# First batch of an attention and two-layer kernel: VectorE's work in one fixed order

## The chip, the cores and the metric

The kernel runs on one core of a Trainium2 chip. The metric is the device time of one execution in microseconds (us). Before the change it is 1152.64 us, the median of three runs (1151.52 to 1152.75). One further execution was recorded by the hardware profiler; all rows below are from it.

The engines carry short names in the rows: PE is TensorE (PEld its weight loads), DVE is VectorE, ACT is ScalarE, POOL is GpSimd, SP is the engine that issues most DMAs.

## What is computed

```
q, k, v: 4 batches x 8 heads x 576 x 64;  tau = 0.02
scores = q @ k^T / 8
keep only scores >= row maximum - tau        (all others: -1e9)
attn = exp(scores - row maximum) / (row sum + 1e-9)
x = attn @ v, heads side by side:            2304 x 512
x = (silu(x @ w_gate) * (x @ w_val)) @ w_out   512 -> 1536 -> 512
out = relu(x @ w_in)^2 @ w_out2                512 -> 2048 -> 512
```

Everything is float32. Most products are made from split operands: a rounded high part and the rest, in three matmuls per product.

## The kernel before, in words

The attention is cut into 144 tiles of 128 query rows by 576 keys: 4 batches, 4 pairs of heads, 9 tiles for a pair. Tiles 0 to 35 are the first batch. In the first batch PE has nothing but the attention; from tile 36 on, the matmuls of the first layer of the batch that is done ("fill") are put between the attention's.

One tile goes through these steps, which the code names by functions:

- QK: four matmuls (eight for the fifth tile of a pair) write the scores `s` into one of two PSUM buffers.
- RED (L623, DVE): the row maximum minus tau, `thr`, read from PSUM.
- CUT (L631, ACT): writes `z` from `s` and `thr`; there is one `z` buffer.
- EXP (L639, ACT): `e = exp(z)` and its row sum. An accumulator read of the same line follows it.
- RCP (L644, DVE): the reciprocal of the sum; NORM (L649, POOL): `e` times it.
- TR (L669, PE): five 128x128 transposes of `e` into two PSUM banks, three columns in one and two in the other.
- PH (L55 in the first batch): copies them to SBUF, one bank by DVE and the other by ACT ("evacuation"). In later batches it is L689 on ACT with a subtraction L61 on DVE.
- AV (L725 in the first batch, L728 later): the product with the values, four times in nine tiles.

Beside this the first layer's weights, which arrive as 64-bit floats, are brought into split 32-bit form: 30 pieces of 128 x 256. A piece takes one step on ACT (L137), four on DVE (L139, L141, L145, L147, each reading what the one before wrote), a copy on ACT (`wa` or `wx`, L53) and a subtraction on POOL (L61). The raw data lies in three buffers, so that three pieces can be under way. A new piece's DMA is started every second tile in the first batch, and every tile later. Twenty pieces carry gate and value weights, the last ten the output weights; the fill needs 20 pieces by its fifth unit and all 30 before its first output (around tile 56).

Each pair of heads also has its q and k split: two conversions on ACT (`land`, L559 and L53), L565 on DVE, two subtractions on POOL; and chunks `xs_m` of the first layer's input are split, L53 on ACT and L61 on DVE.

What sets the order: the program's loop over tiles issues the steps in a written sequence, each through `at_`, which gives it a priority offset from a table ("early0" for the first batch). A scheduler then fixes one order for each engine at build time; on the chip every engine works its list in that order and waits at an instruction whose inputs are missing. In the loop before, the DVE steps of the weights (`loader.tick("D")`, named LD) stand at four places of an iteration, and up to four can be issued in it.

## Time and profile before

| | |
|---|---|
| median of three runs | 1152.64 us |
| the profiled execution | 1153.14 us, of which the recorded span is 1151.3 us |
| DVE busy over the span | 874.8 us (76%) |
| PE busy over the span | 1115.7 us (97%) |
| first batch (tile 0's maximum to tile 36's) | 7.24 to 102.74 us |

A busy share over the whole span mixes stages with different limits, so the views below are cut by stretches of tiles. "Busy" of an engine counts the time in which an instruction of it is recorded as running; this takes in time in which a running instruction is held up. In a timeline row the bracket at the end, where there is one, gives the idle time before the instruction and what ended it.

### The profile page before, as it was taken

The page shows a single profiled execution, that of the slowest core. Times are in us where ns is not written, and L with a number is a line of the kernel's source. Part 1 is how long each engine was busy: PE and PEld are TensorE (multiplying, and loading weights), DVE is VectorE, ACT ScalarE, POOL GpSimd, SP SyncE. Part 2 cuts the span into 40 slices and gives each one's busy share as a digit, 9 for nine tenths or more (in the row PEclk, how much of TensorE's full clock was granted, in tenths as well). Part 3 has the DMA queues.
Part 4 walks back from the last instruction along what each step waited for, and adds up shares of the span by engine and source line. Part 5 has one row for each costly group of instructions (what it writes and reads, how often), then busy time and mean ns, then how long its engine had stood idle before and what let it go on. Part 6 is the DMA issues. An engine that isn't in the chain of part 4 may idle for free.

```text
span 1151.3 us, 19654 instructions
## 1 busy us (share of the span) xinstructions
PE 1115.7 (97%) x6572; PEld 1011.6 (88%) x6572; DVE 874.8 (76%) x2143; ACT 689.2 (60%) x1626; POOL 242.8 (21%) x363
## 2 busy tenths in 40 slices
PE   7888999999999999999999999989999999999998
PEld 5766989999999999998888888889898998899997
DVE  7999997877877773889986888668648767866554
ACT  7988988988888883554443444235546555543221
POOL 5565664555455531000000000000000000000000
PEclk9999999999999999999999999989999999999999
DMA  6666433443333400332220234246364445444542
GB/s 195 193 178 166 128 99 95 100 120 95 95 95 95 105 22 1 101 93 82 83 74 1 73 131 161 91 143 244 137 210 174 174 157 177 153 155 138 187 171 80
DMA packets 55827, 143.15 MB, mean 124 GB/s; under 512 B 7600, under 2 KB 8880, under 8 KB 55728
## 3 DMA queue, kind: packets, MB, share of 16 engines
q1 hardware_dynamic: 55584, 141.92, 39.8%
q8 instruction: 52, 0.85, 0.3%
q14 instruction: 47, 0.39, 0.1%
q10 hardware_dynamic: 144, 0.00, 0.0%
HBM read 93.06 MB, written 22.28 MB: 100 GB/s over the span
## 4 chain that ended last, share of the span: by engine, by line
PE 76%; DVE 12%; ACT 5%; DMA 2%; issue 2%; POOL 0%; POOLq 0%; DVEq 0%; ACTq 0%; SPq 0%
PE mm L226 17%; PE mm L1453 17%; PE mm L1400 13%; PE mm L271 8%; PE bank L226 6%; PE bank L669 4%; PE s L613 4%; PE bank L271 4%; PE bank L728 4%; DVE st__101 L623 2%; DMA wr<-in_w_dram 1%; ACT z L631 1%; DVE pt L61 1%; ACT e L639 1%; DVE xs_m L61 1%
## 5 line engine op out<-in xcount | busy, mean ns | idle before, releaser
L669 PE MATMUL bank<-ident,e 128*128 128x128 f32 x720 | 165.4, 275 | 10.2 <-DVE x L55 3.8
L649 POOL TENSOR_SCALAR e<-e,r 128x576 f32<-128x576 f32 x144 | 113.4, 787 | 148.1 <-DVE r L644 104.6
L61 DVE TENSOR_TENSOR pt<-bank,pt 128x384 fp32r<-128x384 f32 x216 | 100.3, 486 | 51.1 <-ACT pt L689 49.9
L226 PE MATMUL mm<-xs,wa 128*128 128x512 f32 (+2 forms) x672 | 125.7, 347 | 0.5 <-ACT x L53 0.5
L226 PEld LDWEIGHTS mm<-xs,wa 128*128 128x128 f32 x672 | 109.5, 188 | 15.7 <-ACT x L53 0.7
L631 ACT ACTIVATE z<-s,thr 128x576 f32<-128x576 f32 x144 | 106.8, 742 | 26.5 <-DVE st__101 L623 18.5
L623 DVE TENSOR_SCALAR_CACHE_REDUCE st__101<-s,tau_c 128x576 bf16<-128x576 f32 x144 | 116.6, 810 | 5.2 <-PE s L613 4.2
L669 PEld LDWEIGHTS bank<-ident,e 128*128 128x128 f32 x720 | 96.4, 141 | 21.7 <-DVE x L55 5.9
L226 PE MATMUL bank<-xs_m,wa 128*128 128x288 f32 x576 | 109.7, 327 | 3.7 <-DVE xF L740 1.8
L689 ACT ACTIVATE pt<-bank 128x384 fp32r<-128x384 f32 x216 | 88.7, 436 | 21.5 <-PE bank L669 20.2
L639 ACT ACTIVATE e<-z 128x577 f32<-128x577 f32 x144 | 99.6, 692 | 1.5 <-POOL e L649 0.4
L226 PEld LDWEIGHTS bank<-xs_m,wa 128*128 128x128 f32 x576 | 89.0, 189 | 7.1 <-DVE xs_m L61 2.7
L728 PE MATMUL bank<-pt,vs 128*128 128x256 f32 (+1 forms) x480 | 92.1, 323 | 2.1 <-ACT pt L689 1.4
L613 PE MATMUL s<-kh,qs 128*128 128x288 f32 x256 | 78.1, 319 | 7.4 <-ACT nident L413 5.9
L728 PEld LDWEIGHTS bank<-pt,vs 128*128 128x128 f32 x480 | 73.9, 190 | 3.8 <-ACT pt L689 2.1
L1470 DVE TENSOR_TENSOR xF<-xF,mm 128x512 f32<-128x512 f32 x54 | 37.0, 686 | 50.9 <-PE mm L1453 50.9
L226 PE MATMUL mm<-xs,wb 128*128 128x512 f32 (+1 forms) x360 | 74.9, 368 | 0.0
L613 PE MATMUL s<-kl,qs 128*128 128x288 f32 x256 | 73.7, 301 | 0.0
L226 PEld LDWEIGHTS mm<-xs,wb 128*128 128x128 f32 x360 | 62.9, 188 | 11.3
L53 ACT ACTIVATE wb<-wf 128x256 fp32r<-128x256 f32 x82 | 34.0, 414 | 64.5 <-DVE wf L1057 38.4
L1054 ACT ACTIVATE wf<-wr 128x256 f32<-128x256 f32 x64 | 27.6, 433 | 68.6 <-DMA wr<-in_w_dram 51.0
L1453 PE MATMUL mm<-wb,wx 128*128 128x512 f32 x270 | 67.1, 389 | 0.0
(156 smaller groups left out, 2603.0 us busy)
## 6 DMA issues: line engine op xcount, KB each, us to landing
wr<-in_w_dram SPq DMA_DIRECT2D x106, 256.0 KB, 2.9
raw<-in_qkv_dram SPq DMA_DIRECT2D x15, 896.0 KB, 4.7
kh<-land SPq DMA_DIRECT2D x60, 144.0 KB, 2.6
kl<-raw SPq DMA_DIRECT2D x60, 144.0 KB, 2.8
xF<-in_w_dram SPq DMA_DIRECT2D x30, 256.0 KB, 2.9
right<-kept1T SPq DMA_DIRECT2D x8, 768.0 KB, 5.3
right<-kept0T SPq DMA_DIRECT2D x7, 768.0 KB, 5.3
right<-kept SPq DMA_DIRECT2D x6, 768.0 KB, 5.1
```

The source lines that it names most:

```text
L61: e.tensor_tensor(out, a, b, op=ALU.subtract)
L226: mm(pt[:, :n], w[:, a, col + c * P : col + (c + 1) * P], xs[:, b, c, :], start=(i == 0), stop=(i == len(TERMS) - 1),)
L271: mm(pt[:, :n], w[:, a, 2 * DM + m * P : 2 * DM + (m + 1) * P], u[:, b, :], start=(k == 0), stop=(k == last),)
L613: mm(sp[:, cols], l, r[:, cols], start=(n_ == 0), stop=(n_ == len(pairs) - 1),)
L623: red = nc.vector.tensor_scalar(st_, st[t]["s"][:, :S], scalar1=tau_c, scalar2=None, op0=ALU.subtract, op1=ALU.max, accum_out=th)
L631: nc.scalar.activation(z[:, :S], st[t]["s"][:, :S], AF.Prelu, bias=st[t]["thr"], scale=-1.0, alpha=1 / SLOPE)
L639: ex = nc.scalar.activation(e, st[t]["z"], AF.Exp, scale=-SLOPE, accum_out=sum_)
L649: nc.gpsimd.tensor_scalar(e, e, scalar1=r, scalar2=1.0, op0=ALU.mult, op1=ALU.mult)
L669: mm(dst[:, j], e[:, c0 : c0 + P], ident, is_transpose=True, start=(j == 0), stop=(j == len(cols) - 1),)
L728: mm(o[:, :n], hd["vs"][:, SLOT[k % 5], :], pt[:, k, lo : lo + n], start=(k == 0), stop=(k == 9))
L1400: mm(bank[:, :BK], w[:, a, c * P : (c + 1) * P], t[:, b, c, :], start=(n == 0 and x in ("11", "12", "S1")), stop=(n == 5), skip_group_chec ...
L1453: mm(pt, u[:, b, s * P : (s + 1) * P], w[a], start=(half == 0 and j == 0 and i == 0), stop=(half == 1 and j == 1 and i == 2),)
```

## The change

For iterations 9 to 37 of the loop over tiles, the DVE steps are chained: each of them is issued after the DVE instruction that was traced before it (`inorder`). The written sequence of such an iteration i is: reciprocal of tile i-1, maximum of tile i, evacuation of tile i-3, two weight steps. The other places of LD are left out in these iterations. Outside of them the loop is as it was; the priorities are the same.

```diff
+    order = {"after": None}
+
+    def inorder(f, *args, name=None):
+
+        if order["after"] is None:
+            at_(f, *args, name=name)
+        else:
+            with tc.issue_after(order["after"]):
+                at_(f, *args, name=name)
+        traced = nc.cur_bb.bb.instructions
+        engine = st[0]["red"].engine
+        order["after"] = next(x for x in reversed(traced) if x.engine == engine)
+
     for i in range(NTILE + lag + 1):
...
-        at_(loader.tick, "D", name="LD")
-        if i < NTILE:
-            at_(RED, i)
+        fixed = cfg["fixed"][0] <= i < cfg["fixed"][1]
+        if fixed:
+            inorder(RCP, i - 1)
+            at_(NORM, i - 1)
+            inorder(RED, i)
             at_(CUT, i)
-        if 0 <= t < NTILE:
-            at_(PH, t)
-            at_(NEG, t)
-        if i < NTILE:
+            inorder(PH, t)
             at_(EXP, i)
-        at_(loader.tick, "D", name="LD")
+            for _ in range(2):
+                inorder(loader.tick, "D", name="LD")
+        else:
...
-        if 0 <= i - 1 < NTILE:
+        if 0 <= i - 1 < NTILE and not fixed:
             at_(RCP, i - 1)
             at_(NORM, i - 1)
-        at_(loader.tick, "D", name="LD")
+        if not fixed:
+            at_(loader.tick, "D", name="LD")
...
-        at_(loader.tick, "D", name="LD")
+        if not fixed:
+            at_(loader.tick, "D", name="LD")
...
+    "fixed": (9, 38),
```

What the scheduler makes of it is shown at three places of DVE's list. In these rows `thr7` is the maximum of tile 7, `r7` the reciprocal of its sum; the copies into `x2` are evacuations; rows from `xF` to `xF` or with `wf2` at L139 to L147 are weight steps (the three raw buffers lie in `xF`).

The first place is DVE from the maximum of tile 5 on. Before:

```order
L623 TENSOR_SCALAR st__101,thr5_257<-s1_109,tau_c_60 128x576
L139 TENSOR_SCALAR xF_64<-xF_64 128x256
L141 TENSOR_SCALAR xF_64<-xF_64 128x256
L145 SCALAR_TENSOR_TENSOR xF_64<-xF_64 128x256
L644 RECIPROCAL r4_264<-sum4_237 128x1
L147 SCALAR_TENSOR_TENSOR xF_64<-xF_64 128x256
L139 TENSOR_SCALAR wf2_80<-wf2_80 128x256
L623 TENSOR_SCALAR st__101,thr6_278<-s0_108,tau_c_60 128x576
L644 RECIPROCAL r5_285<-sum5_262 128x1
L55 COPY x2_65<-bank0_84 128x3x128
```

Now:

```order
L623 TENSOR_SCALAR st__101,thr5_257<-s1_109,tau_c_60 128x576
L644 RECIPROCAL r4_264<-sum4_237 128x1
L623 TENSOR_SCALAR st__101,thr6_278<-s0_108,tau_c_60 128x576
L644 RECIPROCAL r5_285<-sum5_262 128x1
L55 COPY x2_65<-bank0_84 128x3x128
L623 TENSOR_SCALAR st__101,thr7_298<-s1_109,tau_c_60 128x576
```

The weight steps between the maxima of tiles 5 and 7 are gone; the first weight step now stands behind the maximum and the evacuation of tile 12's iteration. Up to the maximum of tile 5 the two lists are the same.

The second place is DVE in the middle of the first batch. Before, tiles 16 to 18:

```order
L623 TENSOR_SCALAR st__101,thr16_546<-s0_108,tau_c_60 128x576
L55 COPY x2_65<-bank0_84 128x2x128
L623 TENSOR_SCALAR st__101,thr17_587<-s1_109,tau_c_60 128x576
L644 RECIPROCAL r15_555<-sum15_529 128x1
L55 COPY x2_65<-bank1_85 128x3x128
L139 TENSOR_SCALAR wf2_80<-wf2_80 128x256
L61 TENSOR_TENSOR xs_m00_1277<-xF_64,xs_m00_1277 128x288
L141 TENSOR_SCALAR wf2_80<-wf2_80 128x256
L644 RECIPROCAL r16_594<-sum16_551 128x1
L145 SCALAR_TENSOR_TENSOR wf2_80<-xF_64,wf2_80 128x256
L147 SCALAR_TENSOR_TENSOR wf2_80<-xF_64,wf2_80 128x256
L139 TENSOR_SCALAR xF_64<-xF_64 128x256
```

Now, tiles 18 and 19:

```order
L644 RECIPROCAL r17_609<-sum17_593 128x1
L623 TENSOR_SCALAR st__101,thr18_612<-s0_108,tau_c_60 128x576
L55 COPY x2_65<-bank0_84 128x3x128
L139 TENSOR_SCALAR xF_64<-xF_64 128x256
L141 TENSOR_SCALAR xF_64<-xF_64 128x256
L644 RECIPROCAL r18_648<-sum18_617 128x1
L623 TENSOR_SCALAR st__101,thr19_651<-s1_109,tau_c_60 128x576
L55 COPY x2_65<-bank0_84 128x2x128
L145 SCALAR_TENSOR_TENSOR xF_64<-xF_64 128x256
L147 SCALAR_TENSOR_TENSOR xF_64<-xF_64 128x256
```

Before, two maxima stand close together and the reciprocal of the earlier tile often behind the later tile's maximum, with a run of weight steps after them. Now every maximum stands right behind the reciprocal of the tile before it, and two steps of one piece stand behind each evacuation.

The third place is DVE where the fixed iterations end. Before, from the reciprocal of tile 35:

```order
L644 RECIPROCAL r35_1153<-sum35_1124 128x1
L623 TENSOR_SCALAR st__101,thr36_1144<-s0_108,tau_c_60 128x576
L55 COPY x2_65<-bank0_84 128x3x128
L623 TENSOR_SCALAR st__101,thr37_1186<-s1_109,tau_c_60 128x576
L55 COPY x2_65<-bank1_85 128x2x128
L644 RECIPROCAL r36_1195<-sum36_1149 128x1
L139 TENSOR_SCALAR xF_64<-xF_64 128x256
L141 TENSOR_SCALAR xF_64<-xF_64 128x256
L145 SCALAR_TENSOR_TENSOR xF_64<-xF_64 128x256
```

Now, from the reciprocal of tile 36:

```order
L644 RECIPROCAL r36_1182<-sum36_1151 128x1
L623 TENSOR_SCALAR st__101,thr37_1185<-s1_109,tau_c_60 128x576
L55 COPY x2_65<-bank1_85 128x2x128
L145 SCALAR_TENSOR_TENSOR xF_64<-xF_64 128x256
L139 TENSOR_SCALAR xF_64<-xF_64 128x256
L147 SCALAR_TENSOR_TENSOR xF_64<-xF_64 128x256
L141 TENSOR_SCALAR xF_64<-xF_64 128x256
L145 SCALAR_TENSOR_TENSOR xF_64<-xF_64 128x256
L55 COPY x2_65<-bank0_84 128x3x128
L644 RECIPROCAL r37_1221<-sum37_1190 128x1
L147 SCALAR_TENSOR_TENSOR xF_64<-xF_64 128x256
L623 TENSOR_SCALAR st__101,thr38_1212<-s0_108,tau_c_60 128x576
```

Here the run of weight steps is longer than it was before. Counted over the whole list: ahead of the maximum of tile 38 there were 22, 22, 22 and 21 instructions of L139, L141, L145 and L147, and now there are 15 of each; ahead of the maximum of tile 57 there are 30 of each in both lists. From there on DVE's and PE's lists agree apart from a few neighbouring rows up to tile 60, and wholly after that.

## Rows read from the trace of the kernel before

**Rows 1.** Page, part 1: busy time, share of the span, instructions.

```profile
PE 1115.7 (97%) x6572; PEld 1011.6 (88%) x6572; DVE 874.8 (76%) x2143; ACT 689.2 (60%) x1626; POOL 242.8 (21%) x363
```

**Rows 2.** Stretches between maxima: length; busy of PE, PEld, DVE, ACT, POOL; clock, DMA.

```profile
10.26:17.01 6.75, 5.69 (x29) 5.25 (x29) 4.68 (x13) 6.25 (x15) 4.67 (x6) 1.00 0.49 180
17.01:28.39 11.38, 10.93 (x65) 8.98 (x65) 10.85 (x31) 10.71 (x28) 6.97 (x10) 1.00 0.70 162
28.39:109.55 81.16, 69.69 (x399) 55.87 (x400) 76.38 (x199) 72.68 (x180) 48.15 (x67) 1.00 0.67 185
109.55:170.64 61.09, 57.34 (x418) 54.19 (x418) 58.38 (x154) 52.92 (x133) 38.74 (x55) 1.00 0.44 115
170.64:400.00 229.36, 226.03 (x1720) 220.21 (x1719) 177.66 (x484) 198.80 (x491) 121.92 (x180) 1.00 0.41 99
```

**Rows 3.** Timeline (start, length, engine, line): the maxima of tiles 9 and 38.

```profile
28.39 0.81 DVE L623 TENSOR_SCALAR_CACHE_REDUCE st__101<-s,tau_c 128x576 bf16<-128x576 f32 x1
...
109.55 0.81 DVE L623 TENSOR_SCALAR_CACHE_REDUCE st__101<-s,tau_c 128x576 bf16<-128x576 f32 x1
```

**Rows 4.** Timeline of VectorE and ScalarE: one tile from reciprocal to reciprocal.

```profile
102.66 0.16 DVE L644 RECIPROCAL r<-sum 128x1 f32<-128x1 f32 x1
102.74 0.80 DVE L623 TENSOR_SCALAR_CACHE_REDUCE st__101<-s,tau_c 128x576 bf16<-128x576 f32 x1
...
103.46 0.55 DVE L55 COPY x<-bank 128x384 f32<-128x384 f32 x1
...
103.64 0.74 ACT L631 ACTIVATE z<-s,thr 128x576 f32<-128x576 f32 x1 [0.17 <-DVE st__101 L623]
...
104.47 0.69 ACT L639 ACTIVATE e<-z 128x577 f32<-128x577 f32 x1
...
105.28 0.16 DVE L644 RECIPROCAL r<-sum 128x1 f32<-128x1 f32 x1 [0.20 <-ACT e L639]
```

**Rows 5.** Timeline of ScalarE: two pairs of CUT and EXP.

```profile
31.12 0.74 ACT L631 ACTIVATE z<-s,thr 128x576 f32<-128x576 f32 x1
...
32.06 0.67 ACT L639 ACTIVATE e<-z 128x577 f32<-128x577 f32 x1
...
59.20 0.74 ACT L631 ACTIVATE z<-s,thr 128x576 f32<-128x576 f32 x1
59.96 0.69 ACT L639 ACTIVATE e<-z 128x577 f32<-128x577 f32 x1
```

**Rows 6.** Lines of ScalarE, 28.39 to 109.55: a pair's conversions.

```profile
L559 ACT ACTIVATE land<-raw,qscale 128x576 fp32r<-128x576 f32 x3 | 2.3, 774 | 0.0
L53 ACT ACTIVATE land<-raw 128x576 fp32r<-128x576 f32 x3 | 2.1, 688 | 0.0
```

**Rows 7.** Timeline of VectorE and GpSimd: a weight piece beside a normalization.

```profile
62.20 0.41 DVE L145 SCALAR_TENSOR_TENSOR wf<-xF,wf 128x256 int32<-128x256 int32 x1
...
78.73 0.28 DVE L139 TENSOR_SCALAR xF<-xF 128x256 f32<-128x256 f32 x1
...
78.99 0.88 POOL L649 TENSOR_SCALAR e<-e,r 128x576 f32<-128x576 f32 x1 [1.21 <-DVE r L644]
...
79.04 0.29 DVE L141 TENSOR_SCALAR xF<-xF 128x256 int32<-128x256 int32 x1
...
79.37 0.77 DVE L145 SCALAR_TENSOR_TENSOR xF<-xF 128x256 int32<-128x256 int32 x1
...
80.17 0.43 DVE L147 SCALAR_TENSOR_TENSOR xF<-xF 128x256 int32<-128x256 int32 x1
```

**Rows 8.** Stretches, VectorE's L139, L141, L145, L147 alone, in this order.

```profile
109.55:170.64 61.09, 3.16 (x8) 1.00 0.44 115
109.55:170.64 61.09, 4.18 (x8) 1.00 0.44 115
109.55:170.64 61.09, 6.21 (x9) 1.00 0.44 115
109.55:170.64 61.09, 3.88 (x9) 1.00 0.44 115
```

More of the change, by code (lines that the diff above doesn't have):

```diff
@@ L852, in attention_moe @@
             at_(loader.start, name="LS")
-        at_(loader.tick, "D", name="LD")
-        if i < NTILE:
-            at_(RED, i)
+        fixed = cfg["fixed"][0] <= i < cfg["fixed"][1]
[3 more added lines that the diff above has]
+            inorder(RED, i)
             at_(CUT, i)
-        if 0 <= t < NTILE:
-            at_(PH, t)
-            at_(NEG, t)
-        if i < NTILE:
+            inorder(PH, t)
             at_(EXP, i)
-        at_(loader.tick, "D", name="LD")
+            for _ in range(2):
+                inorder(loader.tick, "D", name="LD")
+        else:
+            at_(loader.tick, "D", name="LD")
+            if i < NTILE:
+                at_(RED, i)
+                at_(CUT, i)
+            if 0 <= t < NTILE:
+                at_(PH, t)
+                at_(NEG, t)
+            if i < NTILE:
+                at_(EXP, i)
+            at_(loader.tick, "D", name="LD")
         at_(loader.tick, "A", name="LA")
@@ L868, in attention_moe @@
                 avq.append(t)
-        if 0 <= i - 1 < NTILE:
+        if 0 <= i - 1 < NTILE and not fixed:
             at_(RCP, i - 1)
             at_(NORM, i - 1)
-        at_(loader.tick, "D", name="LD")
+        if not fixed:
+            at_(loader.tick, "D", name="LD")
         at_(mp1.flush, "A", name="FA")
@@ L894, in attention_moe @@
                 at_(next, steps, name="PS")
-        at_(loader.tick, "D", name="LD")
+        if not fixed:
+            at_(loader.tick, "D", name="LD")
     while avq or not fstate["end"]:
```

## The prediction

> **What bounds the kernel now.** I read the page's engine totals first, then the stretches between chosen maxima, and last the timeline of single tiles. The totals give PE 97% busy and DVE 76% [rows 1]. That average hides two stages. The stretches in [rows 2] are cut where the maxima (L623) of tiles 2, 5, 9, 38 and 57 start; the columns after the length are the busy times of PE, PEld, DVE, ACT and POOL. From 170.64 on PE is busy 226.03 of 229.36 us: PE sets the pace, DVE is busy 177.66. Ahead of that DVE is the fullest engine: 10.85 of 11.38 us from tile 5 to 9, 76.38 of 81.16 from tile 9 to 38, 58.38 of 61.09 from tile 38 to 57. In the last of these PE is busy 57.34, so both are near their limit there. The lists of the engines are the same again soon after tile 57, and PE then has no room to catch up. So the change is worth what it moves the start of tile 57.
>
> Why DVE is so full is seen in single rows [rows 7]. A weight step L145 took 0.41 us at 62.20, but 0.77 at 79.37: a normalization ran on POOL from 78.99 to 79.87, and the step ended 0.27 us after it. L139 and L141, which had started before it or just with it, took 0.28 and 0.29. A step that meets a POOL operation is held until that one ends.
>
> **The change, part by part.** I price three stretches.
>
> *Tiles 5 to 9.* The weight steps that stood here are gone (the first place of the lists), 3 to 4 of each line. DVE then no longer sets the pace. The nearest rows for tiles without weight steps are tiles 2 to 5: 6.75 us for three, 2.25 a tile [rows 2]. The other end is a tile that waits for the whole chain of the one before, 2.62 (next paragraph), as tile 9 does. I take the middle, 2.43: four tiles in 9.7 instead of 11.38 us, **-1.7** (bounds -2.4 and -0.9).
>
> *Tiles 9 to 38.* Two things happen here. The DVE work falls: 15 pieces instead of 18 to 19, and few of them are held, because POOL's normalization now runs under the maximum and the evacuation. The normalization that a reciprocal sets free lasts about 0.9 us [rows 7]; in that time DVE now does the maximum and the evacuation, 0.80 and 0.55 long [rows 4], and these read PSUM and are not held. The other thing is a new wait. The list now says reciprocal of tile i-1, then maximum of tile i. The reciprocal needs EXP of tile i-1, that needs its CUT, that needs its maximum. So each round is one closed ring through DVE and ACT, and a maximum can no longer be done ahead, as it was before. The ring is read from one tile [rows 4]: reciprocal 102.66, maximum 102.74, CUT 103.64, EXP 104.47, next reciprocal 105.28, which is 0.08 + 0.90 + 0.83 + 0.81 = 2.62 us. The shortest step from CUT to EXP is 0.76 (59.20 to 59.96), which would make the ring 2.55; with another ACT instruction between the two it is 0.94 (31.12 to 32.06) [rows 5].
>
> Under the ring DVE has room: from the start of a maximum to the next reciprocal there are 2.54 us, and maximum, evacuation and two steps of 0.28 + 0.29 or 0.41 + 0.43 [rows 7] need 0.80 + 0.55 + 0.84 = 2.2 at most. So the weight steps are covered by ACT's CUT and EXP, and what was DVE's bound turns into the ring's. What waits behind a late reciprocal is the next maximum, and with it CUT, EXP and the transposes of the next tile.
>
> 29 rounds at 2.62 are 76.0 us. In 11 of them ACT's new list has an instruction between CUT and EXP: 11 x (0.94 - 0.83) = 1.2. From the end of EXP (104.47 + 0.69) to the next CUT (105.28 + 0.08 + 0.90) ACT has 1.1 us a round; its evacuations and weight copies fit, the three pairs' conversions of 0.77 and 0.69 [rows 6] together with these don't. I allow 0.4 us for each of four such rounds and 0.6 for each of the three rounds in which L565 stands between the weight steps, 3.4 in all. That gives 80.6 us against 81.16 [rows 2]: **-0.6**. The ends are 29 x 2.55 = 74.0 (-7.2), and 2.80, the present pace, plus 0.15 a round for waits of PE that the ring doesn't show (+4.3).
>
> *Tiles 38 to 57.* What was left out has to be made up here: all 30 pieces are done by tile 57 in both lists, and at tile 38 there are 15 now where there were 22. That is 27 more weight steps, 6.75 pieces, on the engine that is busy 58.38 of 61.09 us. In this stretch the four lines took 3.16/8, 4.18/8, 6.21/9 and 3.88/9 us [rows 8], 2.04 us a piece. Neighbours that don't depend on one another overlap, as reciprocal and maximum do by 0.08 us [rows 4], so that a piece occupies about 1.7 (2.04 - 4 x 0.08): 6.75 x 1.7 = 11.5. DVE's idle time in the stretch is 2.7 us; I let half of it be filled: **+10.1**. Bounds: a piece of steps that are never held is 0.28 + 0.29 + 0.41 + 0.43 = 1.41 [rows 7], and with all idle time filled 9.5 - 2.7 = +6.8; at 2.04 with none of it filled +13.8. The same pieces bring their ACT copies and POOL subtractions; ACT is busy 52.92 and POOL 38.74 of the 61.09 us, so these lie beside DVE's work. The raw data's DMAs are started by SP when a buffer comes free; in the first batch that is later than before, and three pieces are still under way at any time, so I cost them at nothing. If a load were late for a step, DVE would stand behind it, some tenths of a microsecond a piece.
>
> *Sum.* -1.7 - 0.6 + 10.1 = +7.8 us on the profiled execution's 1153.14 (the span of 1151.3 and 1.8 around it), which is 1160.9. The profiled execution is 0.5 above the median of the runs, so the forecast is **1160 us**, slower by 0.7%.
>
> [...]
>
> **The rivals.**
>
> *Faster.* The relief counts and the repayment is cheap. Rounds at the shortest ring with one instruction between CUT and EXP in 11 of them, 74.0 + 1.2: -6.0. Tiles 5 to 9 at 2.25: -2.4. Added steps that stand in one run behind the same POOL operation are held once and not four times: +6.8, and a third of that, 2.3, lies in time in which DVE would be held anyway. Sum -3.9: 1148.7. For it: DVE's 76.38 us contain much time in which steps were held. Against it: the ring is a sum of dependent steps and none of them gets shorter, and DVE is 96% busy where the steps go. 13%.
>
> *No change.* Rounds at 2.62 with only the 1.2 us added (-4.0), tiles 5 to 9 at -2.4, late weights at +6.8: +0.4, 1153.0. 16%.
>
> *Much slower.* PE's list puts an AV of some 2.5 us and five transposes ahead of the scores of the tile after next. If such a product waits for an evacuation that now comes only behind the maximum, the scores come late and the ring stands still. At the upper end above, 2.95 a round, the sum is -1.7 + 4.3 + 10.1 = +12.7: 1165.3. It decides from where a round with an AV needs more than the 5.2 us of two rings. For it: PE is busy 69.69 of 81.16 us in this stretch. Against it: the scores have two buffers and may be a tile early. 13%.
>
> That the order isn't what the change says is no rival here; the lists show it.
>
> **How the numbers follow.** Forecast 58%, with a range of its own from 1155 to 1165. A difference of 0.2%, 2.3 us, is about what a measurement of this kernel can tell from none. Faster by more than that has 13%, within it 16%, slower 71% (58 and 13). The range from 1150 to 1167 leaves out most of the faster rival and the outer part of the slowest one.
>
> **What the next profile would show.** Tile 9's maximum near 26.7 instead of 28.39 [rows 3]. From there rounds of 2.6 to 2.9 us, each reciprocal ended by a wait for ACT's EXP, DVE with idle time in every round (below 80% busy) and L145 mostly at 0.41. Tile 38's maximum near 107, against 109.55 [rows 3]. From tile 38 to 57 some 71 us, DVE as full as before with 15 pieces in place of 8, and PE with new waits for DVE. Then the same pace as before. I am wrong if tile 57 comes before 168.3: because the rounds run below 2.55, which would break the ring, or because the stretch after tile 38 takes the added steps at less than 1 us a piece.

## The result and the profile after

The changed kernel takes 1167.8 us (median of 4 runs, 1166.9 to 1168.5) against 1152.1 us (1151.2 to 1152.8) on the same chip: 1.36% longer, ratio 1.0136 with a 95% interval from 1.0119 to 1.0154. That is +15.7 us where +7.8 was forecast: 0.8 us above the wider range of 1150 to 1167, and 2.8 above the forecast's own, 1155 to 1165. The profiled execution took 1166.85 us, 1165.0 of it the span. Its totals, the answer to [rows 1], hardly show where the time went:

```profile
PE 1122.8 (96%) x6572; PEld 1013.8 (87%) x6572; DVE 873.2 (75%) x2143; ACT 691.5 (59%) x1626; POOL 240.8 (21%) x363
```

The stretches do. These are cut, as in [rows 2], where the maxima of tiles 2, 5, 9, 38 and 57 start; behind the length are PE, PEld, DVE, ACT, POOL, the granted clock, the DMA share and GB/s:

```profile
10.27:17.59 7.32, 6.44 (x29) 5.93 (x29) 4.86 (x13) 6.03 (x14) 4.45 (x6) 1.00 0.44 145
17.59:27.73 10.14, 9.78 (x57) 8.07 (x58) 5.04 (x18) 9.63 (x25) 4.76 (x8) 1.00 0.61 129
27.73:114.13 86.40, 73.58 (x410) 57.76 (x409) 69.08 (x185) 71.69 (x171) 42.20 (x61) 0.98 0.55 152
114.13:185.59 71.46, 62.12 (x417) 55.81 (x417) 70.04 (x182) 58.16 (x149) 45.50 (x63) 0.98 0.46 132
185.59:415.00 229.41, 226.47 (x1726) 220.91 (x1725) 178.29 (x486) 199.42 (x492) 122.18 (x182) 1.00 0.40 99
```

Against [rows 2]: tile 5 starts 0.58 later (the two lists are the same up to there, and in the runs told below it starts anywhere from 16.7 to 18.1, so this is not put down to the change); tiles 5 to 9 take 10.14 instead of 11.38, **-1.2**; tiles 9 to 38 take 86.40 instead of 81.16, **+5.2**; tiles 38 to 57 take 71.46 instead of 61.09, **+10.4**; from there to the end it is 1.2 less. Together +13.7, the difference of the two spans. The maxima that answer to [rows 3], and that of tile 57:

```profile
27.73 0.82 DVE L623 TENSOR_SCALAR_CACHE_REDUCE st__101<-s,tau_c 128x576 bf16<-128x576 f32 x1
...
114.13 0.81 DVE L623 TENSOR_SCALAR_CACHE_REDUCE st__101<-s,tau_c 128x576 bf16<-128x576 f32 x1
...
185.59 0.81 DVE L623 TENSOR_SCALAR_CACHE_REDUCE st__101<-s,tau_c 128x576 bf16<-128x576 f32 x1
```

The ring is there, as in [rows 4]. In the timeline of tile 27 each step waits for the one before, and the round takes 2.64 us:

```profile
81.38 0.80 DVE L623 TENSOR_SCALAR_CACHE_REDUCE st__101<-s,tau_c 128x576 bf16<-128x576 f32 x1
...
82.28 0.74 ACT L631 ACTIVATE z<-s,thr 128x576 f32<-128x576 f32 x1 [0.77 <-DVE st__101 L623]
...
83.06 0.69 ACT L639 ACTIVATE e<-z 128x577 f32<-128x577 f32 x1
...
83.94 0.16 DVE L644 RECIPROCAL r<-sum 128x1 f32<-128x1 f32 x1 [0.48 <-ACT e L639]
84.02 0.80 DVE L623 TENSOR_SCALAR_CACHE_REDUCE st__101<-s,tau_c 128x576 bf16<-128x576 f32 x1
```

Eleven of the 29 rounds are like it, 2.62 to 2.66 us. The others reach 4.1, and the mean is 2.98; in the kernel before, the time from one maximum to the next ran from 1.06 to 5.91, with a mean of 2.80. I added up, over all 29 rounds, what each of the ring's four steps took beyond the forecast's 0.90, 0.83, 0.81 and 0.08:

```
us beyond 29 x 2.62 = 76.0   CUT late  to EXP  reciprocal late  next maximum   sum
forecast's allowances           1.6      1.2        1.8             -           4.6
changed kernel                  2.9      2.3        4.9            0.4         10.4
```

Two long rounds show how it comes about. In round 26 (timeline) a copy on ACT stands ahead of CUT, and itself waits for PE's transposes; another stands between CUT and EXP; the reciprocal then starts only behind one more copy of ACT, which the profile names as what it waited for:

```profile
78.66 0.38 ACT L53 ACTIVATE x<-bank 128x256 f32<-128x256 f32 x1 [0.78 <-PE bank L669]
...
78.94 0.73 ACT L631 ACTIVATE z<-s,thr 128x576 f32<-128x576 f32 x1
...
79.74 0.43 ACT L53 ACTIVATE xF<-bank 64x320 f32<-64x320 f32 x1
...
80.07 0.67 ACT L639 ACTIVATE e<-z 128x577 f32<-128x577 f32 x1
...
81.30 0.16 DVE L644 RECIPROCAL r<-sum 128x1 f32<-128x1 f32 x1 [1.35 <-ACT x L53]
```

In round 30 (VectorE's timeline) EXP had long been done, and the reciprocal stands behind three steps that were held while POOL worked without a break from 90.67 to 93.63:

```profile
90.87 0.69 DVE L139 TENSOR_SCALAR xF<-xF 128x256 f32<-128x256 f32 x1
91.48 1.43 DVE L565 SCALAR_TENSOR_TENSOR raw<-raw,qscale,land 128x576 fp32r<-128x576 f32 x1
92.83 0.95 DVE L141 TENSOR_SCALAR xF<-xF 128x256 int32<-128x256 int32 x1
93.70 0.15 DVE L644 RECIPROCAL r<-sum 128x1 f32<-128x1 f32 x1
```

L565 takes 0.82 us at 64.25, where POOL is idle (0.00 us busy from 64 to 66), and 1.43 here.

Such holds did not become few in tiles 9 to 38. The maximum and the evacuation now cover POOL's normalization, but POOL's subtraction for a weight piece (L61) follows it and meets the first weight step. L139, 0.28 us when free, took 0.63 in the mean of its 15 rows; 12 of them were over 0.5, and all 12 started after such a subtraction, or one of a pair's, had started and before it ended:

```profile
L139 DVE TENSOR_SCALAR xF<-xF 128x256 f32<-128x256 f32 x10 | 6.7, 670 | 0.0
L139 DVE TENSOR_SCALAR wf<-wf 128x256 f32<-128x256 f32 x5 | 2.7, 545 | 0.0
```

A whole piece took 1.94 us of DVE here, against 2.06 in the kernel before.

Round 37 (4.01 us) is another thing: behind it the fixed order ends, and five weight steps stand ahead of the reciprocal of tile 37 in DVE's list (the third place of the lists). It holds 1.4 of the 10.4 us, and it is 4.0 to 4.2 us long in seven of the other ten runs with a ring too.

The waits of tiles 9 to 38 (us in all, times, longest) name, among others, the ring, PE's transposes behind DVE's evacuations, and ACT's copies behind PE's transposes:

```profile
DVE r L644 <- ACT e L639: 17.1, 22, 1.9
ACT z L631 <- DVE st__101 L623: 8.4, 15, 1.1
...
PE bank L669 <- DVE x L55: 5.3, 7, 1.6
...
ACT x L53 <- PE bank L669: 1.6, 4, 0.8
```

### The profile page after: what moved, and what is told of

Read it like the earlier page. It is cut to its first block, busy times and chain, and to the rows that moved or that the text cites. A ratio compares the mean times of both kernels' runs of the same rounds, so it can differ in the third digit from the quotient of the medians.

```text
span 1165.0 us, 19639 instructions
## 1 busy us (share of the span) xinstructions
PE 1122.8 (96%) x6572; PEld 1013.8 (87%) x6572; DVE 873.2 (75%) x2143; ACT 691.5 (59%) x1626; POOL 240.8 (21%) x363
## 4 chain that ended last, share of the span: by engine, by line
PE 80%; DVE 9%; ACT 4%; DMA 4%; issue 2%; POOL 0%; SPq 0%; POOLq 0%; ACTq 0%; DVEq 0%
PE mm L226 17%; PE mm L1479 17%; PE mm L1426 13%; PE mm L271 9%; PE bank L226 6%; PE bank L669 5%; PE s L613 4%; PE bank L271 4%; PE bank L728 4%; PE bank L725 2%; DVE st__101 L623 2%; DVE pt L61 1%; ACT z L631 1%; DMA raw<-in_qkv_dram 1%; ACT e L639 1%
## 5 line engine op out<-in xcount | busy, mean ns | idle before, releaser
L61 DVE TENSOR_TENSOR pt<-bank,pt 128x384 fp32r<-128x384 f32 x216 | 100.2, 486 | 49.1 <-ACT pt L689 47.5
L226 PEld LDWEIGHTS mm<-xs,wa 128*128 128x128 f32 x672 | 109.5, 188 | 15.7 <-ACT x L53 0.7
L623 DVE TENSOR_SCALAR_CACHE_REDUCE st__101<-s,tau_c 128x576 bf16<-128x576 f32 x144 | 116.5, 809 | 6.0 <-PE s L613 5.2
```

The lines of the kernel that those rows point to most:

```text
L61: e.tensor_tensor(out, a, b, op=ALU.subtract)
L226: mm(pt[:, :n], w[:, a, col + c * P : col + (c + 1) * P], xs[:, b, c, :], start=(i == 0), stop=(i == len(TERMS) - 1),)
L623: red = nc.vector.tensor_scalar(st_, st[t]["s"][:, :S], scalar1=tau_c, scalar2=None, op0=ALU.subtract, op1=ALU.max, accum_out=th)
```

## The experiments

**The square: ring or not, weights late or not.** The first swaps maximum and reciprocal in the fixed order, so that a maximum may again be done ahead:

```
-            inorder(RCP, i - 1); at_(NORM, i - 1); inorder(RED, i); at_(CUT, i)
+            inorder(RED, i); at_(CUT, i); inorder(RCP, i - 1); at_(NORM, i - 1)
```

> Edit: in the fixed range the list says maximum of tile i, then reciprocal of tile i-1 (the two change places); evacuation and two weight steps behind them as in the changed kernel, so the weights stay late (16 pieces ahead of tile 38, against 15). Theory 1, two separate costs (the closed ring sets the rounds of tiles 9 to 38, the late weights the stretch 38 to 57): the maximum can be done ahead again, the rounds fall from 2.98 us to what ACT and DVE need by their busy time (71.69 and 69.08 us for 29 rounds in the changed kernel, 2.4 to 2.6 a round), tiles 9 to 38 take 71 to 77 us instead of 86.4, tiles 38 to 57 stay at 71 to 73, the time is 1152 to 1160. Rival 2, the order of ACT's queue: the copies between CUT and EXP set the rounds, not the reciprocal: tiles 9 to 38 stay above 83, the time is 1164 to 1168. Rival 3, held steps: the normalization now runs beside the weight steps, these are held again (L145 above 0.55 in the mean instead of 0.49) and DVE is full as in the kernel before: about 80 us, 1160 to 1162.

Measured: 1158.6 us, ratio 1.0055 (1.0035 to 1.0076); tiles 9 to 38 take 80.0, as rival 3 had it, not theory 1's 71 to 77 (the time, 1158.6, is in theory 1's range), and the steps are held more (L145 0.64 us in the mean of 15, 0.47 in the changed kernel; a whole piece 2.17 against 1.94). The second is the kernel before with its free order and late weights (the edit in short):

```
+        if name == "LD" and 9 <= i < 38: with tc.issue_after(st[i]["red"]): return f(*args)
-            at_(loader.tick, "D", name="LD")      (two of the four places, tiles 9 to 37)
```

> Edit: the kernel before with its free order, and only the weight steps of tiles 9 to 37 bound behind the maximum of their own tile at two places per tile, so that 15 to 16 pieces stand ahead of tile 38's maximum (22 in the kernel before, 15 in the changed one); no ring. Theory 1: the late weights cost 11 us between tiles 38 and 57 (72 us instead of 61), and the first stretch gives back what DVE no longer does: 6 to 7 pieces at 1.7 us, tiles 9 to 38 in 70 to 75 us instead of 81.2; the time is 1150 to 1156. Rival 2, tiles 9 to 38 are bound by something other than DVE's work (ACT's queue or PE), so nothing comes back there: 79 to 82 us, and the time is 1161 to 1164. Rival 3, late weights are free and the whole loss is the ring's order carried on: tiles 38 to 57 in 61 to 64, the time is 1140 to 1146.

Measured: 1159.7 us, 1.0060 (1.0045 to 1.0075): the stretches of rival 2, the time 1.3 below its range, since tile 9 comes 1.5 us earlier than in the kernel before. The third keeps the ring and frees the weight steps:

```
-            for _ in range(2): inorder(loader.tick, "D", name="LD")
+            (four places per tile, at_(loader.tick, "D", name="LD"), as in the kernel before)
```

> Edit: the changed kernel with reciprocal, maximum and evacuation in the fixed order, but the weight steps free again (four places per tile, not bound): 28 pieces stand ahead of tile 38's maximum, 4 of them ahead of tile 9. Theory 1: the ring stays and DVE gets 13 more pieces in it; its idle time there is 17 us in the changed kernel, 13 pieces at 1.4 to 2.0 us fill it and more: tiles 9 to 38 in 88 to 96 us; tiles 38 to 57, without 13 pieces at 1.7 us, fall from 72 to what PE needs, 55 to 60; the time is 1155 to 1165. Rival 2, weights done early cost the same on DVE wherever they stand, because DVE's work sets the sum of both stretches: tile 57 at 185 to 188 as in the changed kernel, the time is 1166 to 1169. Rival 3, the ring's slack takes them all: tiles 9 to 38 stay at 86, the time is 1150 to 1154.

Measured: 1166.2 us, 1.0113 (1.0098 to 1.0128): the stretches are theory 1's, with the rounds 0.4 us above its range; the time is 1.2 above its range, where rival 2 had it, but tile 57 starts at 183.6, not at rival 2's 185 to 188. The eighth has neither ring nor late weights: the first's order and the third's free steps.

> Edit: the maximum ahead of the reciprocal and the weight steps free again, so neither the ring nor late weights: 24 pieces ahead of tile 38 (22 in the kernel before, 15 in the changed one), 4 ahead of tile 9. It closes the square with the changed kernel (ring, late), the first experiment (no ring, late) and the third (ring, early). Theory 1, two costs of different places: tiles 9 to 38 in 80 to 83 us as in the kernel before, tiles 38 to 57 in 58 to 61; the time is 1150 to 1155. Rival 2, the fixed maximum-reciprocal-evacuation order itself costs even without the ring: tiles 9 to 38 above 85, the time is 1157 to 1162.

Measured: 1151.3 us, 0.9990 (0.9980 to 1.0000), the same as the kernel before within what can be told: theory 1, with tiles 38 to 57 1.2 us above its range. Stretches of the four, tiles 9 to 38 and 38 to 57 (same columns), in the order told:

```profile
26.82:106.85 80.03, 71.68 (x410) 57.94 (x408) 72.67 (x186) 70.46 (x172) 43.30 (x60) 0.98 0.57 159
106.85:176.58 69.73, 62.00 (x416) 56.92 (x417) 68.18 (x180) 57.97 (x149) 45.41 (x64) 0.95 0.49 142
```

```profile
26.87:106.93 80.06, 71.71 (x410) 58.12 (x409) 68.37 (x188) 71.01 (x172) 44.27 (x61) 0.98 0.58 162
106.93:178.10 71.17, 61.84 (x417) 55.66 (x417) 68.42 (x179) 58.97 (x149) 45.55 (x63) 0.98 0.47 136
```

```profile
28.72:125.12 96.40, 73.47 (x400) 57.71 (x401) 82.42 (x226) 77.88 (x193) 50.31 (x72) 0.96 0.61 171
125.12:183.61 58.49, 57.38 (x420) 54.34 (x419) 48.13 (x128) 49.93 (x125) 34.35 (x50) 1.00 0.38 94
```

```profile
28.33:109.40 81.07, 69.32 (x400) 55.83 (x400) 75.49 (x205) 73.80 (x184) 47.74 (x68) 1.00 0.67 188
109.40:171.59 62.19, 58.14 (x420) 54.43 (x420) 57.73 (x148) 52.96 (x134) 37.88 (x54) 1.00 0.42 110
```

The two costs are real, and they don't add. Without the ring, late weights cost 7.3 us (1158.6 - 1151.3). Ahead of tile 38 there are 8 pieces fewer: the 3.5 that stood ahead of tile 9 give back 1.5 us there (28.33 to 26.82), the 4.5 in tiles 9 to 38 give back 1.0, and the 8 cost 7.5 behind tile 38. (These three give 5.0 of the 7.3; the profiled execution of the first experiment was 1.7 us below its median. TensorE's granted clock was 0.95 there from tile 38 to 57, against 1.00 in the eighth, which lies in the 7.5.) With late weights, the ring costs 9.1 (1167.77 - 1158.63). With early weights the ring costs 14.9, because there an early piece is not free: of 13 pieces more ahead of tile 38 some 10 stand in the rounds, which get 10.0 us longer, and the stretch behind them gets 13.0 shorter. The free orders also show that DVE's load did not set the pace of tiles 9 to 38 before. In the second experiment DVE's busy time falls by 8.0 us [rows 2] and the stretch by 1.1; over the kernel before and the first, second and eighth experiments DVE is busy from 68.4 to 76.4 us, and the stretch takes 80.0 to 81.2.

**How much of the long rounds is weight work.** The fourth does one weight step a tile.

```
-            for _ in range(2):
+            for _ in range(1):
```

> Edit: the changed kernel with one weight step per fixed tile instead of two: 10 pieces ahead of tile 38 instead of 15, 29 to 30 at tile 57. Theory 1: the rounds in which DVE overflowed (reciprocal late behind a full list, 3.7 us in six rounds) come down to the ring, ACT has fewer copies: tiles 9 to 38 in 80 to 83 us instead of 86.4; tiles 38 to 57 take 5 more pieces at 1.7 us: 79 to 82 instead of 72.4; the time is 1168 to 1174. Rival 2, a late piece costs nothing (PE or the loads set that stretch): 72 to 74, the time is 1161 to 1164. Rival 3, DVE has no part in the long rounds (they are ACT's alone): tiles 9 to 38 stay at 85 to 87, the time is 1174 to 1178.

Measured: 1180.1 us, 1.0237 (1.0221 to 1.0252). The time is above every range. Tiles 38 to 57 are as theory 1 has them, 80.9 us: 9.4 more for 5 pieces. Tiles 9 to 38 take 87.43, 0.4 above rival 3's range. The reciprocals are nearly on time now (1.5 us late in all, not 4.9), but CUT's lateness grew from 2.9 to 3.3, the step to EXP from 2.3 to 4.9 and the next maximum from 0.4 to 1.8. Other waits took the place: ACT's copies now wait for PE, in the same view as above,

```profile
ACT x L53 <- PE bank L669: 4.2, 5, 2.0
ACT xF L53 <- PE bank L725: 1.7, 3, 0.6
```

Part of this I put down to PE's clock, which the ninth run brought up (below): it was 0.94 in the mean here, 0.98 in the changed kernel. The longest of these waits, 2.00 us at 78.24, ends a stretch with the clock at 0.60 and 0.55 (74 to 78), and CUT is late by more than 1 us only in rounds 26 and 35, both beside a low clock. So this run does not show what half the weight steps are worth at full clock.

The tenth has no weight work in these tiles at all.

```
+        if not fixed:  (each loader.tick);  later steps: issue_after(maximum 37), issue_after(EXP 37)
```

> Edit: the changed kernel with no weight work at all in tiles 9 to 37 (steps on DVE, copies on ACT, subtractions on POOL are all bound behind the maximum of tile 37 or EXP of tile 37): the ring alone, with the conversions of the pairs and PE's list. Everything is computed, only later, so the time is long (over 1185 us, 15 pieces later than in the changed kernel at 1.7 us or more) and says nothing; tiles 9 to 38 are what is looked at. Theory 1, PE's list and the conversions make the rounds longer than 2.62: 83 to 86 us for the 29 rounds instead of 86.4. Rival 2, the weight work does (two copies on ACT and four steps on DVE a piece): 77 to 80 us.

Theory 1 holds: without weight work the ring takes 84.68 us for 29 rounds, more than the kernel before took with 18 pieces in them. The weight work explains 1.7 of the 86.40 us, or somewhat more, since the clock was lower here (0.96, against 0.98). (The whole took 1191.5 us.)

**ACT's list.** The fifth puts EXP right behind CUT and every other ACT instruction behind EXP.

```
             at_(CUT, i)
+            at_(EXP, i)
             inorder(PH, t)
-            at_(EXP, i)
+    (in at_, tiles 9 to 37: every call under tc.issue_after(ACT's instruction before))
```

> Edit: the changed kernel, and ACT's list is fixed too in tiles 9 to 37: CUT and EXP of a tile stand next to one another, and every other ACT instruction of that tile (its evacuation, weight copies, conversions) behind EXP; the ring and the late weights stay (14 pieces ahead of tile 38, against 15). In the changed kernel the 29 rounds take 12.2 us more than the bare ring of 2.56: 2.85 because CUT comes late, 4.07 between CUT and EXP, 4.86 because the reciprocal comes late. Theory 1, ACT's in-order list carries other waits into the ring (a copy that stands between CUT and EXP and itself waits for PE): without it the 4.07 fall below 0.8 and the rounds take 82 to 84 us instead of 86.4, the time is 1162 to 1165. Rival 2, the copies only change their place and CUT comes late instead: 85.5 to 87.5, time 1166 to 1169. Rival 3, evacuations that come later hold PE's transposes, and the scores with them: over 88, time over 1169.

Measured: 1166.0 us (1164.8 to 1172.9), 1.0132 (1.0100 to 1.0164), not told from the changed kernel: rival 2 by its time. Its profiled execution was the longest, 6.9 us above the median, so its stretches are not used; for what it is worth, in it CUT is late by 6.5 us in all (2.9 in the changed kernel) and the step to EXP by 2.5 (2.3), which is rival 2's way and not theory 1's. The sixth and seventh move nine evacuations of ACT to DVE, without and with the ring.

```
+        if 9 <= t < 36 and i in (1, 4, 7): return "DD"      (both halves evacuated by DVE)
```

> Edit: the first experiment (maximum ahead of the reciprocal, late weights), and in three of nine tiles from 9 to 35 the evacuation that ACT did (0.49 us for three blocks) is done by DVE: some 9 copies, 4.4 us off ACT and 4.5 us onto DVE. In the first experiment tiles 9 to 38 took 80.0 us with ACT busy 70.5 and DVE 72.7; the experiment with late weights alone took 80.1 with ACT 71.0 and DVE only 68.4, and the kernel before 81.2 with ACT 72.7 and DVE 76.4. Theory 1, ACT's in-order list, not DVE, sets the pace of a free order (its busy time and its waits together make 79 of 80 us): tiles 9 to 38 fall by 3 to 5 us, to 75 to 77, the time is 1153 to 1156. Rival 2, DVE sets it: 82 to 85 us, time 1161 to 1164. Rival 3, PE or the loop of the tile as a whole (scores, maximum, CUT, EXP, normalization, transposes with two score buffers and three e buffers) sets it, and no engine's load: 79.5 to 80.5, the time is 1158 to 1159.

> Edit: the changed kernel with the same 9 evacuations moved from ACT to DVE; ring and late weights kept. Theory 1, a round is the longest of the ring, ACT's work in it and DVE's work in it: where a round had nothing but the ring (2.62) nothing changes, DVE's added 0.46 us a round fits in its wait for EXP (0.4 to 1.1 us) except in the rounds that already overflow; rounds with a copy between CUT and EXP get shorter by 0.2: tiles 9 to 38 in 84.5 to 87 us, the time is 1165 to 1168. Rival 2, ACT's total load sets the rounds here as in the free order: 4 us less, 82 to 83, time 1163 to 1164. Rival 3, DVE's list does: 89 to 91, time 1170 to 1172.

Measured: 1165.7 us, 1.0114 (1.0099 to 1.0129), tiles 9 to 38 in 82.85; and 1169.2 us, 1.0145 (1.0128 to 1.0162), in 88.18. In both it got longer, so ACT's load alone doesn't set the pace in either order. Without the ring the stretch is in the range of rival 2, DVE, and the time 1.7 above it; but DVE was busy 74.75 us there, less than the 76.38 of the kernel before, which took 81.16 [rows 2], so it is not the sum of DVE's work. With the ring the result lies between theory 1 and rival 3.

**Conversions and PE.** The fourteenth gives the pairs' conversions to POOL; the ninth leaves out four of the five matmuls of each product with the values, so that PE has little to do there (in short).

```
-        if cfg["qs"] == "A":                     ops.copy(cfg["kh"], kh, k)
+        if cfg["qs"] == "A" and not 2 <= p < 5:  ops.copy(cfg["kh"] if not 2 <= p < 5 else "P", kh, k)
-            for k in range(5):       (ninth, products of tiles 9 to 34)
+            for k in range(1):
```

> Edit: the changed kernel, and for the three pairs whose data are converted in tiles 9 to 38 POOL does the two conversions (L559, L53 land<-raw) that ACT did at 0.76 and 0.67 us. The six rounds with a conversion took 4.7 us more than the ring's 2.62 in the changed kernel, and 2.9 in the run without weight work. Theory 1, they hold CUT and EXP on ACT: tiles 9 to 38 fall to 82.5 to 84.5 us, the time is 1164 to 1166. Rival 2, POOL's conversions hold the normalization and DVE's steps instead: 86 to 88, the time is 1167 to 1169.

Measured: 1168.1 us, 1.0146 (1.0128 to 1.0164); tiles 9 to 38 in 87.22, rival 2. The six rounds 12, 13, 21, 22, 30 and 31 took 20.1 us together before the edit (4.4 above six rings of 2.62, not 4.7 as expected) and 20.2 after it.

> Edit: the changed kernel, and in the 11 products with the values (AV) of tiles 9 to 34 four of the five matmuls are left out, so that the attention output of these tiles is not the reference's; their evacuations, the ring and the late weights stay. It takes about 2.4 us of PE off each, some 26 us of PE's 73.6 in tiles 9 to 38. Theory 1, PE's uneven list holds the ring: the transposes stand between or behind the five matmuls of a product, the evacuation on ACT or the e buffer waits for them, and CUT and EXP come late: the rounds without a conversion fall to 2.62 to 2.70 and those with one (six) keep some 4.7 us together; tiles 9 to 38 take 79.5 to 82 us instead of 86.4. Rival 2, ACT's and DVE's own uneven work holds it: 85 to 87 us. The part past tile 38 stays at 70 to 73 in either case.

Measured: 1170.6 us, 1.0150 (1.0135 to 1.0165); 86.75 for tiles 9 to 38, in rival 2's range, and 77.50 behind them, not 70 to 73. It can't decide, because it changed more than it took away: the granted clock was 0.84 in the mean, and the transposes that were left ran slower (325 ns in the mean, 285 in the changed kernel). That led to the clock. In the changed kernel (2 us stretches, columns as above) PE is busy 3.00 of the 6 us from 68 to 74; then the clock is 0.50, where the kernel before has 1.00 throughout [rows 2]:

```profile
68.00:70.00 2.00, 1.18 (x9) 0.89 (x7) 2.00 (x4) 1.29 (x4) 1.83 (x4) 1.00 0.75 215
70.00:72.00 2.00, 1.21 (x9) 1.09 (x9) 1.49 (x5) 1.64 (x5) 0.48 (x1) 1.00 0.46 98
72.00:74.00 2.00, 0.61 (x5) 0.41 (x3) 1.86 (x5) 0.94 (x3) 1.44 (x2) 0.92 0.38 131
74.00:76.00 2.00, 2.00 (x9) 1.54 (x8) 1.33 (x6) 1.62 (x5) 0.62 (x1) 0.50 0.01 4
```

The thirteenth keeps PE busy there, with scores computed twice. In the changed kernel the copy on ACT that waited 0.78 us for transposes, at 78.66, stands in round 26, which took 3.62 us; rounds 25 and 26 took 6.25 together, 1.0 more than two rings of 2.62.

```
+        again = 9 <= t < 38 and t % 9 in (0, 2, 4, 6, 7)
+        halves_ = [slice(0, HS)] * (1 + again) + [slice(HS, S)]
```

> Edit: the changed kernel, and for 16 of the 29 tiles from 9 to 37 (those without a product of the values beside them) PE computes the scores' first half twice, with the same result: two more matmuls of 0.29 us each, some 9.5 us of PE in all. [...] Theory 1, the ring's idle PE loses its clock and a slow stretch costs the ring about 1.3 us: the clock stays at 1.00 from tile 9 to 38, round 25 and 26 together lose 1.0 to 1.3 us, tiles 9 to 38 take 84.8 to 85.6 us instead of 86.4. Rival 2, the clock costs the ring nothing (the AV would be late at full speed too): 86 to 87. Rival 3, scores come late by the added work: over 87.5.

Measured: 1163.5 us, 1.0100 (1.0085 to 1.0115), below the changed kernel's interval although PE does more. PE is busy 4.74 of the 6 us from 68 to 74, and the clock stays at 1.00 in tiles 9 to 38:

```profile
26.89:111.73 84.84, 75.52 (x448) 61.73 (x447) 68.63 (x184) 71.71 (x171) 42.46 (x61) 1.00 0.57 158
...
74.00:76.00 2.00, 2.00 (x11) 1.34 (x10) 1.34 (x5) 1.89 (x5) 0.21 (x1) 1.00 0.94 205
```

Tiles 9 to 38 lose 1.6 us; rounds 24 to 26, beside the slow stretch, lose 0.7 of it (9.16 to 8.42), and rounds 25 and 26 lose 0.5, less than theory 1's 1.0 to 1.3; no run shows 1.3 us for a slow stretch. Tile 9 was 0.8 us earlier too, which the edit doesn't explain: in the fourteen runs without a weight step ahead of it, it starts between 26.57 and 27.73, and the changed kernel's profiled execution is the latest. The fifteenth and sixteenth put these together on the ring without weight work: conversions on POOL, then the repeated scores as well.

> Edit: the run without weight work in tiles 9 to 37, and these three pairs' conversions on POOL. What remains in the rounds is the ring (2.66), copies of ACT between CUT and EXP and PE. Theory 1: 84.7 less the 2.9 us that its six conversion rounds had above 2.66: 81.5 to 82.5 us for tiles 9 to 38. Rival 2, POOL's conversions hold as much: 84 to 86. The whole time says nothing, since the weights are late.

> Edit: the last one, and the scores' first half of 16 tiles computed twice, so that PE keeps its clock. In the run without weight work the clock was 0.50 in two stretches (70 to 74 and 98 to 101 us), and round 35 waited 1.86 us for a copy behind a product at the low clock. Theory 1: the clock stays at 1.00, rounds 26 and 35 lose 1.2 to 1.8 us together: 79.8 to 81 us for tiles 9 to 38, near 29 rounds of 2.66 (77.1) and some 3 us of copies between CUT and EXP. Rival 2, the products are late at full speed too: 81.5 to 82.5. The whole time says nothing.

Tiles 9 to 38 of the run without weight work, and of it with the conversions on POOL:

```profile
26.57:111.25 84.68, 75.18 (x416) 59.36 (x415) 44.53 (x127) 64.60 (x147) 32.11 (x48) 0.96 0.46 119
```

```profile
26.81:109.16 82.35, 71.91 (x416) 57.27 (x415) 45.62 (x127) 60.68 (x141) 37.14 (x54) 1.00 0.48 122
```

82.35 is where theory 1 had it, but for another reason than it gave: the conversion rounds (12, 13, 20, 21, 29 and 30) lost 0.7 us, and rounds 26 and 35 lost 1.6; these two stood beside a clock of 0.50 in the tenth run, and here the clock stayed at 1.00. In these 82.35 us the ring is nearly alone: 29 rounds of 2.66 (77.1), 2.7 for ACT's copies between CUT and EXP, and two long rounds, 29 (1.0, the reciprocal behind L565, which had waited 1.2 for POOL's conversion) and 37 (1.5, the end of the fixed order). With repeated scores it took 83.23, since the scores of tiles 13 and 31 then came late (1.0 and 0.7): neither theory's number. The thirteenth and the sixteenth both have repeated scores and a clock of 1.00, and differ by 1.6 us (84.84 and 83.23): that is what weight work and conversions are worth together, as far as these runs tell.

**A version that gains?** Two tries with a new load at every tile instead of every second one: the first's order with three bound steps, and the eighth's.

```
-    "lev": 2,
+    "lev": 1,
```

> Edit: the first experiment (maximum, reciprocal, evacuation in a fixed order, the weight steps bound to their tile) with a new load started at every tile instead of every second one and three weight steps a tile instead of two: 22 pieces ahead of tile 38 as in the kernel before, none ahead of tile 9. Theory 1, early tiles without weights keep the 1.5 us gained ahead of tile 9, the free order takes 7 more pieces at 0.1 to 0.5 us each in tiles 9 to 38 (80.0 us with 15), tiles 38 to 57 take 60 to 62 us: tile 57 at 168 to 172, the time is 1148 to 1153. Rival 2, bound steps meet the normalization and DVE is full: tiles 9 to 38 in 86 to 90 us, the time is 1155 to 1160.

> Edit: the eighth experiment (maximum, reciprocal, evacuation in a fixed order, weight steps free) with a new load started at every tile instead of every second one: 29 pieces ahead of tile 38 instead of 24. Theory 1, an early piece is cheap without the ring (0.1 to 0.5 us) and a late one dear (0.9 to 1.7): tiles 9 to 38 in 81.5 to 84 us instead of 81.1, tiles 38 to 57 in 57.5 to 59 instead of 62.2: the time is 1148 to 1151, below the kernel before. Rival 2, ACT and DVE are full in tiles 9 to 38 at 24 pieces already, 5 more cost 1.4 to 2 us each there: 88 to 91 us, the time is 1154 to 1158.

Measured: 1158.7 us, 1.0048 (1.0032 to 1.0063), tiles 9 to 38 in 86.37; and 1154.6 us, 1.0011 (1.0002 to 1.0021):

```profile
28.31:115.84 87.53, 69.04 (x400) 56.13 (x400) 83.83 (x227) 77.43 (x193) 54.29 (x73) 1.00 0.64 185
115.84:173.53 57.69, 56.92 (x420) 54.44 (x419) 48.30 (x127) 50.00 (x125) 33.07 (x49) 1.00 0.40 102
```

Rival 2 in the first; in the second its rounds nearly (88 to 91 expected) and theory 1's 57.7 behind them. 5 pieces more than the eighth cost 6.5 us here and give back 4.5 behind tile 38. Some 22 to 24 pieces ahead of tile 38 (18 to 20 of them in tiles 9 to 38) are what a free order takes nearly for nothing; the kernel before has 22. No version beat it by more than can be told.

## Why the prediction was wrong

*Direction and places* were right: three stretches, the ring of 2.62 in place of DVE's list, late weights paid for behind tile 38, the old pace after tile 57.

*Tiles 5 to 9*, -1.7: measured -1.2, within its bounds; tile 5 itself came 0.6 later, which is within what it varies from run to run (16.7 to 18.1).

*Tiles 38 to 57*, +10.1: measured +10.4. A late piece took 2.04 us of DVE (four lines, 15 or 16 times each), as in the forecast, and DVE's idle time went from 2.7 to 1.4, the half that was assumed. The four lines, as in [rows 8]:

```profile
114.13:185.59 71.46, 6.05 (x15) 0.98 0.46 132
114.13:185.59 71.46, 7.54 (x15) 0.98 0.46 132
114.13:185.59 71.46, 9.51 (x15) 0.98 0.46 132
114.13:185.59 71.46, 7.99 (x16) 0.98 0.46 132
```

The clock's mean of 0.98 lies in it as well; how much of the 10.4 is that, no run separates.

*Tiles 9 to 38*, -0.6: **the step that failed**, measured +5.2, beyond its upper bound of +4.3. The ring's length was right; what failed is the sentence that ACT's evacuations and weight copies fit into its 1.1 us a round, with 3.4 us allowed for the rest and 1.2 for instructions between CUT and EXP. 10.4 was needed, and each of the three allowances was too small (1.6, 1.2 and 1.8 against 2.9, 2.3 and 4.9). A premise of the last one failed as well, that few weight steps are held under the ring: L139 took 0.63 us in the mean, not 0.28, and two steps were priced at 0.84 at most. What the runs put in their place:

- Not mainly the weight work: without any of it the rounds still took 84.68 us, or 83.1 without what rounds 26 and 35 lost beside a low clock.
- The closure of the ring. The first experiment removes only that, and tiles 9 to 38 fall by 6.4 us with nearly the same work and the same mean clock (0.98). My reading is that a closed ring makes each round the longest of what three in-order lists need in that round, where the free order let a long round borrow from short ones: none of the changed kernel's rounds is below 2.62, and the kernel before had rounds from 1.06 to 5.91.
- Easing one list gave nothing. Half the weight steps took 3.4 us off the late reciprocals, and 4.4 came back at the other three steps, with ACT's waits for PE up from 1.6 to 5.9, part of it, as I read it, by the clock (0.94 in the mean, not 0.98); copies moved to DVE and conversions moved to POOL gained nothing.
- PE's granted clock fell for some microseconds (0.50 from 74 to 76, 0.72 from 76 to 78); in the run with repeated scores it stayed at 1.00, and tiles 9 to 38 lost 1.6 us. The free orders with late weights have this too (0.98 in the first and second experiments), so it is not the ring's alone.
- The end of the fixed order, which stood in the lists and was not priced: 1.4 us in round 37.

The comparison was off too. I read DVE's 76.38 busy of 81.16 us as what set that stretch before; the second experiment refutes it. ACT was busy 72.68 there too [rows 2]; what did set the pace no run singles out. Of the 6.75 pieces that were moved, 3.5 had stood ahead of tile 9, and what they cost came back in tiles 5 to 9 (-1.2). The other 3.25 had cost little in tiles 9 to 38 (1.0 us for 4.5 of them, first against eighth), so their going could not pay for the ring.

*The rivals.* "Much slower" had the place and nearly the price (2.95 a round; measured 2.98), but its mechanism, late scores, is not what happened: L623 never waited for PE in the changed kernel's tiles 9 to 38. What its first half said did: transposes waited 5.3 us for DVE's evacuations, and in round 26 the delay reached the ring through a copy of ACT (ACT's copies waited 1.6 us for transposes in all). I gave it 13%, having priced the ring's neighbours by their sum and not round by round. "Faster" is refuted by the tenth run: with the weight work gone altogether the rounds were still longer than before. The signs of being wrong that I gave looked to that side only, at a tile 57 before 168.3; it came at 185.6, and no sign stood on the side where the error was.

*Open.* What sets the 80 to 81 us of the free orders; why the clock stayed at 1.00 in the fifteenth run and fell in the tenth and the fourteenth; what PE's products alone cost the ring; and how the 10.4 us divide among the causes above, since most runs that ease one of them also change the clock.

## What to carry to other kernels

Before fixing an order, look for a cycle in it: an instruction that waits for another engine, placed ahead of the one that starts this engine's next round, closes a ring, and then, as I read these runs, every unevenness of each list is paid in full, round by round, instead of being averaged over buffers (29 rounds took 86.40 us with the ring and 80.03 without it, in the first experiment). Price such a ring as the sum over rounds of the longest list, not as the longest sum (a proposal: it was not tried out on these lists). And an engine that is 94% busy, as DVE was in tiles 9 to 38 before, need not be the one that sets the pace: take work off it before you count on its relief.

## What the runs showed of the hardware

I had not expected TensorE's clock to matter in a stretch in which PE is 85% busy; in the kernel before it was 86% busy there, and the clock stayed at 1.00. So the mean did not tell these two apart. In the changed kernel the granted clock was at 0.50 from 74 to 76, after 6 us in which PE had been busy for 3.00, and was up again (0.72 from 76 to 78, then 1.00) while PE worked without a break, 6.00 of the 6 us from 74 to 80. In the 6 us from 68 to 74 PE was busy 5.29 in the kernel before and 4.74 in the thirteenth run, and there the clock stayed at 1.00. Two matmuls of a product with 320 columns took 1.27 us together in the slow part and 0.70 behind it:

```profile
75.92 1.27 PE L725 MATMUL bank<-x 128*128 128x320 f32 x2
...
77.16 0.70 PE L725 MATMUL bank<-x 128*128 128x320 f32 x2
```

What sets the clock no run shows by itself. In this kernel a change that only moves PE's waits came with a slower PE, and a kernel with two more matmuls in 16 tiles beat the changed one (1.0100 against 1.0136), though 0.8 us of that lies ahead of the tiles that were edited.
